# Dense matrix products as eight 64x32 tiles in an attention-and-feed-forward kernel on one Trainium2 core

## The chip, the core and the metric

The kernel runs on one core of a Trainium2 chip. The metric is the device time of one execution in microseconds, as the median of several runs. A profile is one further execution, taken apart by the hardware profiler; it has its own time, and its span runs from its first to its last instruction.

The engines are named as in the profile: PE is TensorE, and PEld its weight loads; DVE is VectorE, ACT ScalarE, POOL GpSimd, and SP is SyncE, which here issues most DMAs. A matrix product takes a stationary operand (the weights, loaded by a weight load) and a moving operand that is streamed past it. Its sums go to one of eight PSUM banks. The array of 128x128 cells can be used as smaller tiles that work beside each other: 64x128 means two tiles of 64 rows, 64x32 means eight tiles, 32x64 eight of another shape.

## The reference

The input x has 2048 rows of 448. It is normalized by row, and a sliding attention and a feed-forward network both read the normalized rows. Their product is added to x.

```python
def _A_ref(x, wqkv, wo):                 # H = 16 heads of 28
    W, dil = 8, 2
    qkv = (x @ wqkv)...                   # 448 -> 3*448
    idx = pos[:, None] - (jnp.arange(W) * dil)[None, :]
    logits = einsum("bhsd,bhswd->bhsw", q, k[idx]) * Dh ** -0.5   # masked where idx < 0
    o = einsum("bhsw,bhswd->bhsd", softmax(logits), v[idx])
    return o.reshape(B, S, D) @ wo
def _B_ref(x, w1, b1, w2, b2):            # 448 -> 1792 -> 448
    return gelu(x @ w1 + b1) @ w2 + b2
xn = _layernorm(x)
return x + _A_ref(xn, ...) * silu(_B_ref(xn, ...))
```

All data is bfloat16. Since the attention looks back in steps of two, even and odd rows never meet; the kernel keeps all even rows first and all odd rows after them.

## The kernel before

The 2048 rows are 16 tiles of 128 (index t) in four chunks of 512 (index c). Attention works in nine blocks (VIS) of four windows of 57 queries (56 in the middle block), each window with 64 keys.

The kernel doesn't write its order down by hand. Every step is a task with an engine, a cost, its dependencies, the buffers that it takes and gives back, and a priority. `_Plan.run` simulates the engines with these costs and picks, among the tasks that can start nearly first, the one with the highest priority; the tasks are then emitted in the order found. HOP (0.10 us) is the planner's time from one engine to another, and SWITCH (0.095 us) what it charges when PE goes to another tile shape (`mode`). The priorities are tables of numbers (PRIO, LATER). PE, like every engine, works through its tasks in the emitted order.

The steps on PE are these. `project` makes q, k and v: `qk_rows` (L532) and `vproj` (L556). `ff1` (L591) makes the first layer, 128 hidden units for 512 rows at a time, and ACT applies gelu (L595). Both have a contraction of 448 = 3.5 x 128. They run in `pair`, as row halves: two products share the array, one on rows 0 to 63 into one bank and the other on rows 64 to 127 into another bank; then the halves are swapped, and each product is finished in the same bank by the other half of the rows. Between the two phases a `nop` on POOL or SP waits for the last products of the first phase, and the second phase waits for the `nop`, since two row halves must not write one bank at the same time. `ff2_part` (L627) makes the second layer for one row tile with 14 products of 128x128, and `final_part` (L796) the output projection with four of them. The last row tile is worked in two halves of 224 columns.

Scores (L677) are 64 small products of 57 columns in tiles of 32x64, into four banks. P V (L709) is 64 products of 57 columns in tiles of 64x32, into two banks. `VISITS` joins them: a visit is P V of one block and, right behind it, the scores of the block two further on. Between scores and P V lie the exponential on ACT (L687) and the mask (L693), which the planner gives to DVE or POOL. After P V, DVE turns the sums (L719), inverts the row sums (L723), turns them back (L728) and multiplies (L733).

After the second layer come the bias (L649, DVE), tanh (L655, ACT) and the gate (L659, DVE); after the projection the product with the gate (L801, DVE), the sum with x (L807, DVE or POOL for the first eight row tiles, DVE for the others) and the output's DMA on SP (L811). POOL issues the DMAs that gather v for the blocks (L354), and SP the transposing loads of the normalized rows and of q and k (L360).

Of the kernel before, what the change touches and what calls it, by code (L numbers as in the profile page):

```python
# [16 lines left out]
SWITCH = 0.095  # L17
TILED = 30
SAME = 20
HOPS = ("POOL", ("SP", "POOL"))  # L20
MASK_ON = (("DVE", "POOL"), (0.4, 1.2))


def VISITS(bs):
    out = [[("S", b)] for b in bs[:2]]
    for i, b in enumerate(bs):
        out.append([("P", b)] + [("S", c) for c in bs[i + 2:i + 3]])
    return out
# [11 lines left out]
class _Task:  # L40
    __slots__ = ("eng", "cost", "deps", "fn", "prio", "take", "give", "slots",
                 "start", "end", "on", "ndep", "users", "tail", "seq", "table", "limit", "mode", "out")


class _Plan:
# [7 lines left out]
    def add(self, eng, cost, fn, deps=(), prio=0, take=(), give=(), tail=0.0, table=(), limit=None,  # L53
            mode=128):
# [5 lines left out]
        t.mode, t.out = mode, None  # L60
# [14 lines left out]
    def _at(self, t, e, free):  # L75
        at = free.get(e, 0.0)
        for p, n in t.take.items():
            if len(p.free) < n or p.fifo and p.fifo[0] is not t:
                return None
            at = max(at, sorted(p.free)[n - 1][0] + HOP)  # L80
        if t.table and self.table not in t.table:
            at += TABLE
        for d in t.deps:
            at = max(at, d.end - d.tail if d.on == e else d.end + HOP)
        if e == "PE" and t.mode != self.mode:
            at = max(at, free.get(e, 0.0) + SWITCH)
        return at

    def run(self):
# [6 lines left out]
        self.mode = 128  # L96
        ready = [t for t in self.tasks if not t.ndep]
        order = []
        while ready:
# [14 lines left out]
            tiled = first[2] == "PE" and self.mode < 64  # L114
            at, t, e, c = min(near, key=lambda k: (-k[1].prio - (TILED if tiled and k[1].mode < 64 else SAME if k[2] == "PE" and k[1].mode == self.mode else 0),
# [4 lines left out]
            if e == "PE" and t.fn is not None:  # L120
                self.mode = t.out or t.mode
# [43 lines left out]
def kernel(  # L165
# [80 lines left out]
    def ring(name, n, shape, dt=BF16, fifo=False):  # L246
# [24 lines left out]
        "project": (49.5, 205, 104, 52.5,),  # L271
        "project2": (147, 150, 101, 61,),
        "values": (89.5, 62.5, 21, 58,),
        "attn": (185, 179.5, 78, 174.5, 106.5, 106, 138.5, 136.5, 32.5,),
        "ff1": (185, 180, 84.5, 176.5, 66.5, 64.5, 156.5, 189.5, 203, 146, 76, 114.5, 77.5, 179.5,
            75.5, 118.5, 180.5, 14.5, 163, 68, 151, 115.5, 194.5, 167.5, 180, 188.5, 86, 93,),
        "gelu": (62.5, 22.5, 95, 92.5,),
        "ff2": (144, 162.5, 103.5, 142.5, 44.5, 112.5, 67, 5, 89, 106.5, 101.5, 75, 74, 55, 11.5,
            6.5,),
        "final": (140, 19.5, 70.5, 47, 112, 34.5, 23.5, 142.5, 73, 53, 198.5, 188.5, 81.5, 126.5,  # L280
            180, 71,),
        "norm": (37.5, 132, 179.5, 129.5, 74.5, 99, 161, 69, 63, 62, 43.5, 73, -5.5, 90, 133.5,
            150,),
        "loads": (166.5, 166, 188, 139.5, 54.5,),
        "stats": (47.5, -60, 180.5, 23, 127, 56, 188.5, 77, 197.5, -13.5, 185, 205.5, 138, 14, 52.5,
            138.5,),
        "turn_x": (108.5, -1, 28, 116, 210, 116.5, 131.5, 160, 41.5, 79.5, 70, 119, -4.5, 74.5,
            132.5, 111,),
        "turn_qk": (68.5, 112, 174.5, 90, 80, 6, 149.5, 60.5, 4, 140.5, 199.5, 96.5, 103, 166.5,
            140, 156,),  # L290
        "move_v": (81.5, 95, 23, 95, 18.5, 26.5, 8, 128, 29.5,),
        "copies": (50, 119.5, 58.5, 76, 32.5, 135.5, 43, 1, 87, 79.5, 129, 77, 32, 41.5, 135,),
    }
    LATER = {"swap": 135, "qk": 165, "v": 29.5, "gelu": 30.5, "exp": 55.5, "mask": -60, "pv": 45, "recip": -16.5, "os": 54.5, "y": 153.5, "tanh": 182.5, "g": 58, "sg": 183, "o": 120.5}
# [50 lines left out]
    def dma(eng, dst, src, kb, prio, deps=(), issue=0.5, rate=350.0):  # L345
# [3 lines left out]
        return plan.add("DMA", kb / rate, lambda _: None, [a], prio, tail=1.7)  # L349
# [16 lines left out]
    def load_x(t0, n, prio, eng="SP", deps=()):  # L366
        d = dma(eng, x_sb[:, t0:t0 + n, :],
                rows(x_half, t0 * P, n * P).rearrange("(t p) d -> p t d", p=P), 112 * n, prio, deps,
                rate=270.0 if t0 < TPC else 350.0)
# [11 lines left out]
    def load_w(kt, prio):  # L381
        t_w.append([dma("SP", w_in[:, kt, :], A_wqkv[kt * P:(kt + 1) * P, :], 336, prio, rate=270.0)])
# [6 lines left out]
    t_w.append([dma("SP", w_in3[:64], tails[:, 0:3:2, :], 112, PRIO["loads"][3], rate=270.0),  # L389
                dma("SP", w_in3[64:], tails[:, 1:3, :], 112, PRIO["loads"][3], rate=270.0)])  # L390

    t_b1z = plan.add("POOL", 0.1, memset("gpsimd", b1r[:], 0.0), [t_on], prio=99)
    t_b1r = dma("POOL", b1r[:NMT], B_b1.rearrange("(m f) -> m f", f=P), 4, 94.5, [t_b1z])
    t_b1r.tail = 5.0
# [74 lines left out]

    def together(top, bottom):  # L470
        return [(f(), g()) for f, g in zip(top, bottom, strict=True)]
# [5 lines left out]
    def pair(a, b, prio, early=False):  # L477
# [11 lines left out]
        def f2(k):  # L489
            held["told"] = (nc.gpsimd if k.on == "POOL" else nc.sync).nop()  # L490
            for i in held["last"]:
                behind(held["told"], i)
        told = plan.add(HOPS[0] if early else HOPS[1], 0.06, f2, [t], 300)

        def f3(k):
            p, q = buf(p_b, t, 0), buf(p_b, t, 1)
            for i in together([part(b, q, kt, 0, kt + 4) for kt in range(3)], [part(a, p, kt, 1, kt + 4) for kt in range(3)])[0]:
                behind(i, held["told"])
# [5 lines left out]
    def first_batch(tiles, prio, tiles0=0):  # L504

        f = []
        for kt in range(3):
            for i, js in enumerate(tiles):
                def f1(k, kt=kt, i=i, js=js):
                    for q, j in enumerate(js):  # L510
                        j.part(buf(p_b, f[i] if kt else k, q), kt, 2, kt == 0, False)
# [14 lines left out]
    def qk_rows(t, which, prio):  # L526
        cs = slice(t * P, (t + 1) * P)

        def part(ps, kt, half, start, stop):
            r = half_rows(half)  # L530
            w = w_in[r, kt, which * D:(which + 1) * D] if kt < 3 else w_in3[r, 0, :]
            return nc.tensor.matmul(ps[:, :D], xnT[r, kt, cs], w, start=start, stop=stop)  # L532

        def evac(a, own, i):
# [6 lines left out]
            if len(t_row[t]) == 2:  # L541
                t_qk[t] = dma_T(qkT[:, :, :, cs].rearrange("p w g c -> p (w g) c"), lambda: b[:].rearrange("p w h c -> p (w h c)"),
                                t_row[t], PRIO["turn_qk"][t], None, 2, 1.9 if t < 3 else 3.8 if t == TPC else 2.0 if t == TPC + 1 else 1.27)
# [6 lines left out]
    def vproj(t, prio):  # L550
        k0 = t * P

        def part(ps, kt, half, start, stop):
            r = half_rows(half)
            w = w_in[r, kt, 2 * D:] if kt < 3 else w_in3[r, 1, :]
            return nc.tensor.matmul(ps[:, :D], xnT[r, kt, k0:k0 + P], w, start=start, stop=stop)  # L556
# [7 lines left out]
    def values(b):  # L564

        t_v[b], v_at[b] = [], []
        for i in range(2):
            first = None
            for w in range(2):
                k0 = VIS[b][2][w][i][1]  # L570
                for lo in sorted({k0, max(k0, (k0 + NK - 1) // P * P)}):
# [6 lines left out]
                    t_v[b].append(d)  # L578
# [6 lines left out]
    def ff1(c, mt, prio, gate):  # L585
# [3 lines left out]
        def part(ps, kt, half, start, stop):  # L589
            r = half_rows(half)  # L590
            return nc.tensor.matmul(ps[:], w1[r, kt, ms], xnT[r, kt, cs], start=start, stop=stop)  # L591
# [18 lines left out]

    def ff2(t, prio):
        t_g[t] = []
        for cs, n, end in parts(t):
            ff2_part(t, cs, n, end, prio - 0.1 * end)

    def ff2_part(t, cs, n, end, prio):
# [23 lines left out]
        a = halves[1]  # L640
        t_f2[t] = a

        if t == NT - 1:
            prio += 9
        if biased:
            y, pool, held = halves[0], p_b, ((p_b, halves[0], 0),)
        else:
            def f2(k):
                nc.vector.tensor_tensor(out=buf(p_y, k)[:, :n], in0=buf(p_b, halves[0])[:, :n], in1=b2[:, cs], op=ALU.add)  # L649
            y, pool = plan.add("DVE", dve(n), f2, [a, t_b2], prio + LATER["y"], take=(p_y,), give=((p_b, halves[0], 0),)), p_y  # L650
# [15 lines left out]
    def scores_of(b):  # L666
        q, nq, wins = VIS[b]

        def fn(banks):
            for i in range(2):  # L670
                for g in range(G):
                    for hl in range(4):
                        for w in range(2):
                            r = slice(32 * hl, 32 * hl + 32)
                            q0, k0 = wins[w][i]
                            c0 = (G * i + g) * nq
                            nc.tensor.matmul(banks[hl][NK * w:NK * w + NK, c0:c0 + nq], qkT[r, 1, g, k0:k0 + NK],  # L677
                                             qkT[r, 0, g, q0:q0 + nq], start=True, stop=True)
# [288 lines left out]
```

## Time and profile before

| | |
|---|---|
| median of three runs | 157.52 us (157.37 to 158.0) |
| the profiled execution | 157.98 us |
| its span | 156.2 us |
| TensorE clock granted | 1.00 throughout |
| PE busy | 150.1 us, 2204 products |
| DVE, ACT, POOL busy | 113.2, 83.3, 74.7 us |

The lines of the profile give the source line, the engine, the operation, the tiles written and read, the shape and the count. For products, "64*128 64x512" is the tile shape and the moving operand. In a timeline, a line begins with the start and the length in us of a merged stretch. Products overlap, and their ends are modelled, so the step from one to the next is read from the starts. In a line of the windows view the columns are the stretch, its length and each engine's busy time with its number of instructions.

### The profile page before, as it was taken

How to read it: one execution, taken by the hardware profiler on the slowest of the kernel's cores; microseconds unless marked ns; L12 is line 12 of the kernel's file. 1: busy time of each engine (PE TensorE's matmuls, PEld its weight loads, DVE VectorE, ACT ScalarE, POOL GpSimd, SP SyncE). 2: the span in 40 equal slices, each digit the busy share in tenths (PEclk: the TensorE clock that was granted, in tenths of full speed). 3: DMA queues.
4: the chain of work that ended last, by engine and by line, in shares of the span. 5: the costliest groups of instructions: out<-in, count | busy, mean ns of one | idle time of the engine just before them, and what ended most of it. 6: DMA issues, size and time to landing. Idle time of an engine off the chain costs nothing.

```text
span 156.2 us, 5305 instructions
## 1 busy us (share of the span) xinstructions
PE 150.1 (96%) x2204; PEld 77.8 (50%) x2204; DVE 113.2 (72%) x259; ACT 83.3 (53%) x149; POOL 74.7 (48%) x123
## 2 busy tenths in 40 slices
PE   6999999999999999999999999999999999999980
PEld 2544454444455555455554644455556444545570
DVE  4789551486266758997799895109899996998992
ACT  3245867378889416444634149782496587051220
POOL 7854856000459408839261098389599780000000
PEclk9999999999999999999999999999999999999999
DMA  4999969999749443099039822123300100200211
GB/s 156 329 317 315 167 124 187 237 269 307 141 95 166 64 82 90 10 192 138 4 83 85 131 70 73 38 76 83 105 0 4 34 31 29 63 4 0 68 36 43
DMA packets 33575, 17.36 MB, mean 111 GB/s; under 512 B 25331, under 2 KB 32387, under 8 KB 33552
## 3 DMA queue, kind: packets, MB, share of 16 engines
q1 hardware_dynamic: 31472, 14.03, 41.3%
q0 software_dynamic: 1936, 2.88, 8.5%
q8 instruction: 17, 0.28, 0.8%
q10 hardware_dynamic: 144, 0.11, 0.2%
q14 instruction: 6, 0.05, 0.1%
HBM read 7.06 MB, written 1.84 MB: 57 GB/s over the span
## 4 chain that ended last, share of the span: by engine, by line
PE 80%; DVE 8%; DMA 3%; POOL 2%; issue 2%; ACT 1%; SPq 1%; DVEq 0%; ACTq 0%; POOLq 0%
PE bank L627 23%; PE bank L591 22%; PE bank L532 11%; PE bank L796 7%; PE bank L556 6%; PE bank L677 4%; PE bank L709 4%; PE bank L327 3%; DMA xnT<-xn 3%; POOL v L354 2%; DVE sg L801 2%; DVE o L807 1%; DVE w_in L659 1%; ACT E L687 1%; DVE xn L438 1%
## 5 line engine op out<-in xcount | busy, mean ns | idle before, releaser
L627 PE MATMUL bank<-w,h 128*128 128x448 bf16 (+1 forms) x238 | 45.2, 342 | 0.0
L591 PE MATMUL bank<-xnT,w 64*128 64x512 bf16 x392 | 44.7, 376 | 0.0
L595 ACT ACTIVATE h<-bank,b 128x512 bf16<-128x512 f32 x56 | 34.0, 689 | 12.9 <-PE bank L591 12.8
L354 POOL DMA_DIRECT2D v<-v_tok x52 | 27.6, 538 | 19.8 <-PE bank L709 9.0
L693 POOL TENSOR_TENSOR E<-E,m_gen 128x456 bf16<-128x456 bf16 x24 | 26.7, 1139 | 11.7 <-ACT E L687 9.5
L627 PEld LDWEIGHTS <-h 128*128 128x128 bf16 x238 | 22.3, 98 | 18.1 <-issue 0.4
L591 PEld LDWEIGHTS <-w 64*128 64x128 bf16 x392 | 19.1, 94 | 22.7 <-issue 1.1
L532 PE MATMUL bank<-w_in,xnT 64*128 64x448 bf16 (+1 forms) x212 | 24.3, 350 | 0.1
L687 ACT ACTIVATE E<-bank 128x456 bf16<-128x456 f32 (+1 forms) x36 | 17.0, 555 | 9.1 <-PE bank L677 9.1
L655 ACT ACTIVATE t<-y 128x448 f32<-128x448 f32 x15 | 8.7, 578 | 17.4 <-DVE y L649 17.4
L719 DVE STREAM_TRANSPOSE dt<-bank 128x480 f32<-128x480 f32 (+1 forms) x18 | 12.1, 671 | 5.6 <-PE bank L709 5.6
L532 PEld LDWEIGHTS <-xnT 64*128 64x128 bf16 (+1 forms) x212 | 10.6, 94 | 10.9 <-issue 1.1
L314 DVE CAST qk_tok<-bank 128x448 bf16<-128x448 f32 x16 | 9.4, 613 | 6.8 <-PE bank L532 6.8
L796 PE MATMUL bank<-wo,oT 128*128 128x448 bf16 (+1 forms) x68 | 14.1, 342 | 0.0
L312 ACT CAST qk_tok<-bank 128x448 bf16<-128x448 f32 x16 | 8.3, 533 | 10.6 <-PE bank L532 10.0
L556 PE MATMUL bank<-w_in,xnT 64*128 64x448 bf16 (+1 forms) x106 | 13.4, 349 | 0.0
L649 DVE TENSOR_TENSOR y<-bank,b 128x448 f32<-128x448 f32 x15 | 9.3, 620 | 4.9 <-PE bank L627 4.9
L728 DVE STREAM_TRANSPOSE dt<-rd 128x480 f32<-128x480 f32 (+1 forms) x18 | 12.1, 673 | 0.5
L733 DVE TENSOR_TENSOR oT<-bank,dt 128x456 bf16<-128x456 f32 (+1 forms) x18 | 11.3, 630 | 0.5
L404 DVE BATCH_NORM_STATS2 st<-x_sb 128x6 f32<-128x448 bf16 x16 | 9.6, 603 | 2.4 <-DMA x_sb<-in_A_x_dram 2.4
L438 DVE TENSOR_SCALAR xn<-x_sb,mv,rstd 128x448 bf16<-128x448 bf16 x16 | 6.3, 394 | 6.0 <-POOL rstd L426 5.8
L796 PEld LDWEIGHTS <-oT 128*128 128x128 bf16 x68 | 6.3, 98 | 6.3 <-issue 0.8
(62 smaller groups left out, 128.9 us busy)
## 6 DMA issues: line engine op xcount, KB each, us to landing
out_dram<-o SPq DMA_DIRECT2D x15, 112.0 KB, 1.7
w<-in_B_w_dram SPq DMA_DIRECT2D x2, 784.0 KB, 7.2
w<-in_B_w_dram SPq DMA_DIRECT2D x2, 672.0 KB, 7.0
x_sb<-in_A_x_dram SPq DMA_DIRECT2D x3, 448.0 KB, 6.3
v<-v_tok POOLq DMA_DIRECT2D x20, 64.0 KB, 2.5
w_in<-in_A_wqkv_dram SPq DMA_DIRECT2D x3, 336.0 KB, 4.3
w<-in_B_w_dram SPq DMA_DIRECT2D x4, 112.0 KB, 6.5
wo<-in_A_wo_dram POOLq DMA_DIRECT2D x4, 98.0 KB, 4.2
```

Source lines behind the costliest of these rows:

```text
L354: nc.gpsimd.dma_start(dst(k), src())
L532: return nc.tensor.matmul(ps[:, :D], xnT[r, kt, cs], w, start=start, stop=stop)
L556: return nc.tensor.matmul(ps[:, :D], xnT[r, kt, k0:k0 + P], w, start=start, stop=stop)
L591: return nc.tensor.matmul(ps[:], w1[r, kt, ms], xnT[r, kt, cs], start=start, stop=stop)
L595: nc.scalar.activation(buf(p_h, own, i)[:], buf(p_b, own, i)[:], ACT.Gelu_apprx_tanh, bias=b1[:, mt:mt + 1])
L627: nc.tensor.matmul(ps[:, :n], buf(*h_at[(c, mt)])[:, j * P:(j + 1) * P], w2[:, mt, cs], start=(mt == 0 and not biased), stop=(mt == NMT - 1))
L687: nc.scalar.activation(buf(p_E, k)[:, :n], buf(p_b, a, at + hl)[:, :n], ACT.Exp, scale=SCALE)
L693: (nc.gpsimd if k.on == "POOL" else nc.vector).tensor_tensor(out=E[:, :n], in0=E[:, :n], in1=m[:, :n], op=ALU.mult)
L719: nc.vector.transpose(buf(p_dt, k)[:, :32 * m], buf(p_b, po, i)[:, :32 * m])
L728: nc.vector.transpose(buf(p_dt, d)[:, :32 * m].rearrange("p (b c) -> p b c", c=32), buf(p_rd, r)[:, :m].unsqueeze(2).to_broadcast((P, m, 32)))
L733: nc.vector.tensor_tensor(out=oT[:, :, q0:q0 + 2 * nq], in0=buf(p_b, po, i)[:, :n].rearrange("p (l q) -> p l q", l=4), in1=buf(p_dt, d)[:, ...
L796: nc.tensor.matmul(ps[:, :n], oT[:, kt, t * P:(t + 1) * P], wo[:, kt, cs], start=(kt == 0), stop=(kt == KT - 1))
```

## The change

Nearly all products with a contraction of 64 rows or more now run in the tile shape of P V. `strips` cuts the 128 output columns of a product into four products of 32, and `together` issues those of the two row halves in turn, so that one round is eight products in eight tiles. The second layer and the output projection, which used the whole array, are worked for two row tiles at a time in two phases with the swap and the `nop` of `pair` (`rows_in_pairs`, `ff2_pair`, `final_pair`). The last two row tiles keep the 128x128 form, and so does the first batch of projections except for its last step. The `nop` waits for the last product alone, and only the first product of the second phase waits for the `nop`.

Scores and P V are tasks of their own (`scores`, `attend`), with no fixed order between them but the data; the planner adds APART (0.25 us) when one comes right behind the other, and prefers tasks of the shape that PE has. All masks go to DVE. The sum with x of row tile 14 and of the first half of 15 goes to POOL. The bias of the first layer is loaded earlier, the planner's rates for the first loads are a little higher, and all priorities are new.

```diff
@@ -15,17 +15,11 @@
 SLACK = 0.12
 TABLE = 1.28
 SWITCH = 0.095
-TILED = 30
+APART = 0.25
+OTHER = 0
 SAME = 20
 HOPS = ("POOL", ("SP", "POOL"))
-MASK_ON = (("DVE", "POOL"), (0.4, 1.2))
-
-
-def VISITS(bs):
-    out = [[("S", b)] for b in bs[:2]]
-    for i, b in enumerate(bs):
-        out.append([("P", b)] + [("S", c) for c in bs[i + 2:i + 3]])
-    return out
+MASK_ON = ("DVE", 0.4)
 
 
 class _Pool:
...
@@ -84,7 +78,16 @@
             at = max(at, d.end - d.tail if d.on == e else d.end + HOP)
         if e == "PE" and t.mode != self.mode:
             at = max(at, free.get(e, 0.0) + SWITCH)
+        if e == "PE" and t.thin and self.thin:
+            at = max(at, free.get(e, 0.0) + APART)
         return at
+
+    def same(self, e, t):
+        if e != "PE":
+            return 0
+        if t.mode == self.mode:
+            return SAME
+        return OTHER if self.mode == 32 and t.mode != self.dense else 0
 
     def run(self):
         for t in self.tasks:
...
-            tiled = first[2] == "PE" and self.mode < 64
-            at, t, e, c = min(near, key=lambda k: (-k[1].prio - (TILED if tiled and k[1].mode < 64 else SAME if k[2] == "PE" and k[1].mode == self.mode else 0),
+            at, t, e, c = min(near, key=lambda k: (-k[1].prio - self.same(k[2], k[1]),
                                                    k[0], k[1].seq))
             if t.limit is not None and at > t.limit:
                 t.fn, c = None, 0.0
             t.on, t.start = e, at
             if e == "PE" and t.fn is not None:
-                self.mode = t.out or t.mode
+                self.mode, self.thin = t.mode, t.thin
+                self.dense = t.mode if t.mode != 32 else self.dense
             if t.table and self.table not in t.table:
                 self.table = t.table[0]
             free[e] = at + c
...
     t_b1z = plan.add("POOL", 0.1, memset("gpsimd", b1r[:], 0.0), [t_on], prio=99)
-    t_b1r = dma("POOL", b1r[:NMT], B_b1.rearrange("(m f) -> m f", f=P), 4, 94.5, [t_b1z])
-    t_b1r.tail = 5.0
+    t_b1r = dma("POOL", b1r[:NMT], B_b1.rearrange("(m f) -> m f", f=P), 4, 400, [t_b1z], tail=4.3)
...
@@ -467,8 +469,15 @@
     def half_rows(half):
         return slice(64 * half, 64 * half + 64) if half < 2 else slice(0, P)
 
+    def strips(out, lhsT, rhs, half, start, stop):
+        n = P if half > 1 else 32
+        return [lambda c=c: nc.tensor.matmul(out[c:c + n], lhsT[:, c:c + n], rhs, start=start, stop=stop) for c in range(0, P, n)]
+
     def together(top, bottom):
-        return [(f(), g()) for f, g in zip(top, bottom, strict=True)]
+        done = []
+        for f, g in zip(top, bottom, strict=True):
+            done.append([q() for pair in zip(f(), g(), strict=True) for q in pair])
+        return done
 
     def behind(later, earlier):
         tc.add_manual_dep(later.ins, earlier.ins.name,
@@ -488,14 +497,12 @@
 
         def f2(k):
             held["told"] = (nc.gpsimd if k.on == "POOL" else nc.sync).nop()
-            for i in held["last"]:
-                behind(held["told"], i)
+            behind(held["told"], held["last"][-1])
         told = plan.add(HOPS[0] if early else HOPS[1], 0.06, f2, [t], 300)
 
         def f3(k):
             p, q = buf(p_b, t, 0), buf(p_b, t, 1)
-            for i in together([part(b, q, kt, 0, kt + 4) for kt in range(3)], [part(a, p, kt, 1, kt + 4) for kt in range(3)])[0]:
-                behind(i, held["told"])
+            behind(together([part(b, q, kt, 0, kt + 4) for kt in range(3)], [part(a, p, kt, 1, kt + 4) for kt in range(3)])[0][0], held["told"])
...
-            return nc.tensor.matmul(ps[:], w1[r, kt, ms], xnT[r, kt, cs], start=start, stop=stop)
+            return strips(ps[:], w1[r, kt, ms], xnT[r, kt, cs], half, start, stop)
...
+    def rows_in_pairs(A, B, steps, deps, prio, n, take, give, dep2=()):
+
+        def part(f, half, i):
+            return lambda: f(half, i)
+        ph1, ph2, held = [], [], {}
+        for i, own in enumerate(steps):
+            def f1(k, i=i, own=own):
+                p, q = buf(p_b, (ph1 or [k])[0], 0), buf(p_b, (ph1 or [k])[0], 1)
+                held["last"] = together([part(A(p), 0, m) for m in own], [part(B(q), 1, m) for m in own])[-1]
+            ph1.append(plan.add("PE", pe(n, len(own)), f1, deps[i] + ph1[-1:], prio + 0.5 * i, take=() if i else (p_b, p_b), tail=0.15, mode=64))
+
+        def f2(k):
+            held["told"] = (nc.gpsimd if k.on == "POOL" else nc.sync).nop()
+            behind(held["told"], held["last"][-1])
+        told = plan.add(HOPS[1], 0.06, f2, ph1[-1:], 300)
+        for i, own in enumerate(steps):
+            def f3(k, i=i, own=own):
+                p, q = buf(p_b, ph1[0], 0), buf(p_b, ph1[0], 1)
+                first = together([part(B(q), 0, m) for m in own], [part(A(p), 1, m) for m in own])[0]
+                if not i:
+                    behind(first[0], held["told"])
+            end = i + 1 == len(steps)
+            ph2.append(plan.add("PE", pe(n, len(own)), f3, [told] + ph2[-1:] + list(dep2) * end, prio + LATER["swap"] + 0.5 * i,
+                                give=give if end else (), tail=0.15, mode=64))
+        return ph1[0], ph2[-1]
+
     def ff2(t, prio):
-        t_g[t] = []
-        for cs, n, end in parts(t):
-            ff2_part(t, cs, n, end, prio - 0.1 * end)
+        t_g.setdefault(t, [])
+        if t >= NT - 2:
+            for cs, n, end in parts(t):
+                ff2_part(t, cs, n, end, prio - 0.1 * end)
+        elif t % 2 == 0:
+            ff2_pair(t, prio)
+
+    def ff2_pair(t, prio):
+        c, j = divmod(t, TPC)
+
+        def product(u):
+            def at(ps):
+                def f(half, mt):
+                    r = half_rows(half)
+                    first = (half == u % 2) and mt == 0
+                    last = (half != u % 2) and mt == NMT - 1
+                    return strips(ps[:, :D], buf(*h_at[(c, mt)])[r, (u % TPC) * P:(u % TPC) * P + P], w2[r, mt, :], half, first, last)
+                return f
+            return at
+        last = j == TPC - 2
+        own, a = rows_in_pairs(product(t), product(t + 1), (range(7), range(7, NMT)),
+                               ([t_h[(c, mt)] for mt in range(7)] + t_w2[0] + [ff1_last[c]], [t_h[(c, mt)] for mt in range(7, NMT)] + t_w2[1]),
+                               prio, D, 2, tuple(h_at[(c, mt)] for mt in range(NMT)) if last else (), [t_f2[q] for q in range(c * TPC, t)] if last else ())
+        t_f2[t] = t_f2[t + 1] = a
+        t_g[t + 1] = []
+        for i in range(2):
+            gate(t + i, slice(0, D), D, own, i, a, prio, False)
...
+    last_visit = {"S": None, "P": None}
+
+    def visit(what, fn, deps, prio, n, give):
         def f1(k):
-            for fn in fns:
-                fn(k)
+            for i in range(2):
+                fn([buf(p_b, k, j) for j in range(n)], i)
+        a = plan.add("PE", 0.5, f1, deps[0] + deps[1] + [last_visit[what]], prio, take=(p_b,) * n, give=give[0] + give[1], tail=0.15,
+                     mode=32 if what == "S" else 64, thin=True)
+        last_visit[what] = a
+        return a, a
+
+    def scores(b, early, gate):
+        fn, deps = scores_of(b)
         prio = PRIO["attn"][b]
-        a = plan.add("PE", cost, f1, deps, prio + (LATER["pv"] if what[0][0] == "P" else 0), take=take, give=give, tail=0.15,
-                     mode=32 if what[0][0] == "S" else 33)
-        a.out = 32 if what[-1][0] == "S" else 33
-        at, exps = 0, []
-        for w, blk in what:
-            last_visit[w].append(a)
-            if w == "S":
-                state[blk] = weights_of(blk, a, at, PRIO["attn"][blk], state["gate"])
-                exps += state[blk][0]
-                at += 4
-            else:
-                for w in range(2):
-                    output_of(blk, a, at + w, w, PRIO["attn"][blk])
-                at += 2
-        return exps
-
+        a, z = visit("S", fn, [d + early for d in deps], prio, 4, ((), ()))
+        return weights_of(b, a, z, prio, gate)
+
+    def attend(b, exps, masked):
+        fn, give = values_of(b, exps)
+        prio = PRIO["attn"][b]
+        a, z = visit("P", fn, [masked + t_v[b][0], t_v[b][1]], prio + LATER["pv"], 2, (tuple(v_at[b][:1]), give + tuple(v_at[b][1:])))
+        for w in range(2):
+            output_of(b, a, z, w, prio)
...
     def final(t, prio):
+        if t < NT - 2:
+            if t % 2 == 0:
+                final_pair(t, prio)
+            return
         for i, (cs, n, end) in enumerate(parts(t)):
             final_part(t, cs, n, t_g[t][i], prio - 0.1 * i)
+
+    def final_pair(t, prio):
+        def product(u):
+            def at(ps):
+                def f(half, kt):
+                    r = half_rows(half)
+                    return strips(ps[:, :D], oT[r, kt, u * P:(u + 1) * P], wo[r, kt, :], half, half == u % 2 and kt == 0, half != u % 2 and kt == KT - 1)
+                return f
+            return at
+        own, a = rows_in_pairs(product(t), product(t + 1), (range(KT),), (t_oT[t] + t_oT[t + 1] + t_wo + [t_f2[t]],), prio, D, 2, ())
+        for i in range(2):
+            close(t + i, slice(0, D), D, t_g[t + i][0], own, i, a, prio)
...
-        o = plan.add(("DVE", "POOL") if t < 2 * TPC else "DVE", (dve(n, 2), 1.15) if t < 2 * TPC else dve(n, 2), f3, [s], prio + LATER["o"], take=(p_o,), give=((p_sg, s, 0),))
+        o = plan.add("POOL" if t == NT - 2 or t == NT - 1 and not cs.start else ("DVE", "POOL") if t < 2 * TPC else "DVE",
+                     0.1 + n / 420 if t == NT - 2 or t == NT - 1 and not cs.start else (dve(n, 2), 1.15) if t < 2 * TPC else dve(n, 2), f3, [s], prio + LATER["o"], take=(p_o,), give=((p_sg, s, 0),))
...
-                state["gate"], state["early"] = gels, gels[:-1]
-                for what in visits(run):
-                    exps += attn(what[0][1], what)
+                done = [(b, *scores(b, gels[:-1], gels)) for b in run]
+                for b, e, m in done:
+                    attend(b, e, m)
+                    exps += e
```

The calls of `qk_rows` and `vproj` are changed as that of `ff1` (its two lines with `ps[:]` above). The tables PRIO and LATER have new numbers throughout, which are left out here.

## The prediction

> **What bounds the kernel now.** I read the page first.
>
> ```profile
> PE 150.1 (96%) x2204; PEld 77.8 (50%) x2204; DVE 113.2 (72%) x259; ACT 83.3 (53%) x149; POOL 74.7 (48%) x123
> ...
> q8 instruction: 17, 0.28, 0.8%
> ...
> PE 80%; DVE 8%; DMA 3%; POOL 2%; issue 2%; ACT 1%; SPq 1%; DVEq 0%; ACTq 0%; POOLq 0%
> ```
>
> TensorE is busy for 96% of the span and carries 80% of the chain that ended last. The waits of PE add to 0.2 us after its start. So a gain must come out of PE's own order and modes, and a loss must make PE slower or make it wait. The timeline of PE shows what its time is made of:
>
> ```profile
> 84.85 1.69 PE L796 MATMUL bank<-wo,oT 128*128 128x448 bf16 x8
> 86.38 1.49 PE L627 MATMUL bank<-w,h 128*128 128x448 bf16 x7
> 87.79 0.68 PE L709 MATMUL bank<-E,v 64*32 64x57 bf16 x64
> 88.40 0.78 PE L677 MATMUL bank<-qkT 32*64 32x57 bf16 x64
> 89.11 1.50 PE L627 MATMUL bank<-w,h 128*128 128x448 bf16 x7
> 90.45 0.92 PE L796 MATMUL bank<-wo,oT 128*128 128x448 bf16 x4
> 91.30 0.93 PE L556 MATMUL bank<-w_in,xnT 64*128 64x448 bf16 x8
> ```
>
> Read the starts. Eight products of 128x128 take 86.38 - 84.85 = 1.53 us, 0.19 each (448 columns). The seven after them take 1.41, where 7 x 0.19 = 1.33: the step into the 64x32 shape costs some 0.09. The four L796 at 90.45 take 0.85 instead of 0.76 before the shape 64x128: again 0.09. I use 0.095 for a change of tile shape. P V costs 0.61 and the scores behind it 0.71, the step out included. A scores visit that stands alone is cheaper:
>
> ```profile
> 48.94 0.70 PE L677 MATMUL bank<-qkT 32*64 32x57 bf16 x64
> 49.57 8.12 PE L627 MATMUL bank<-w,h 128*128 128x448 bf16 x42
> ```
>
> That is 0.63 from start to start. How fast the array takes 64x32 tiles is seen at the head of a P V visit, in a narrow window of the timeline (73.36 to 73.491):
>
> ```profile
> 73.37 0.30 PE L709 MATMUL bank<-E,v 64*32 64x57 bf16 x32
> ```
>
> 32 products, four rounds of eight tiles, each tile with its own weights, began in 0.12 us: 30 ns a round. 57 columns stream in 57/448 x 189 = 24 ns, so weight loads and issue together cost at most 6 ns a round beyond the stream. A whole visit has 64 in 0.61 us, at worst 9.5 ns each, 76 ns for eight.
>
> Then the windows by stage, for the engine that may come next:
>
> ```profile
> core 0: us, PE busy (x) PEld busy (x) DVE busy (x) ACT busy (x) POOL busy (x), PEclk, DMA share, GB/s
> ...
> 62.00:92.00 30.00, 30.00 (x594) 16.00 (x590) 27.03 (x51) 12.94 (x26) 14.90 (x16) 1.00 0.59 94
> ...
> 104.00:153.40 49.40, 47.47 (x794) 26.12 (x788) 43.45 (x80) 23.57 (x41) 20.80 (x26) 1.00 0.14 41
> ```
>
> DVE is at 90% from 62 to 92 and at 88% from 104 to its last instruction; from 144.68 on the chain of waits runs through it. It has little room.
>
> **Part 1, mode changes.** Following the tile shapes down the PE timeline from 45 us to the end I count 37 changes. After: only scores leave the 64x32 shape (nine visits, two steps each, 18), and the last two row tiles' second layer and output projection keep 128x128 (one step in, one reserve): 20. 17 x 0.095 = -1.6 us. If the planner mixes the last two tiles with other work, some steps come back; if two scores visits touch, two go. The start, until 13 us, keeps its five.
>
> **Part 2, scores and P V apart.** P V had a step in and was followed by scores. Scores behind P V took 0.69, 0.75, 0.63, 0.71 and 0.63 against 0.63 alone: 0.25 us in all. The second of two P V visits in a row, at 104.63 and 132.52, took 0.15 more each than 0.61 less its step. Apart, both go: -0.55 us.
>
> **Part 3, the dense work as eight tiles.** 392 and 300 row-tiled products (196 and 150 rounds), 196 of the second layer's (14 of 16 tiles) and 56 of the output projection become 598 rounds of eight, some 6,040 products in all instead of 2,204. A round streams the same columns as the step it replaces: 189 ns, or 216 for 512 columns. The trace has no such tile with a long stream. From below I know no reason why a round should be faster than its stream: 0. From above: 6 ns a round, as P V shows at most, is 3.6 us. I take 0, since the 6 ns were seen where a load must fit into 24 ns, and here it has 187. Issue needs 76 ns a round and is hidden by the stream of 187. Instructions: 0.28 MB in 17 blocks is 16 KB, 256 instructions; 0.8% of 16 engines' span is 1.2 us a block. After, a block lasts 16 rounds, 3.0 us, so fetching has 2.5-fold room; scores alone already eat half a block in 0.63 us with no wait. Nothing. But a visit leaves the queue empty, and the next dense round then starts its eighth tile 60 ns late (76 less what two tiles need), which is paid when the shape is next drained: nine scores visits, +0.5 us.
>
> One rule speaks against this part. By the Trainium skill (TensorE: Matmul & The Clock Gate, Back-to-back and "Wait — 56ns"), matmul starts never come closer than about 25 ns; eight would need 200 ns, 11 more than a 448-column step, and over 402 such rounds the sum would be 4.4 us worse. The row above, 32 starts in 0.12 us, does not agree, and the measurement decides. The same skill (TensorEngine Tiling, Restrictions) says that column tiling switches off the fast weight load, and the page named before it (LDWEIGHTS) gives columns/1.2 ns for one load, 27 ns for 32 columns: eight strictly in turn would be an estimated 213 ns, 24 more, 9.6 us in the 402 rounds. Again the window, with 32 loads and products in 0.12 us, says otherwise.
>
> **Part 4, the swap of row halves.** Second layer and projection now run in two phases, with a hop over SP or POOL between (14 new ones). The first layer and the projections have such hops, and PE shows no wait at any, since other work is put between; the cover is other PE work of the same shape. Uncovered, a hop is two semaphore steps at the planner's 0.1 (HOP) and its nop's 0.06, 0.26; 14 of them are 3.6 us. If SP is in a transposing load's issue (1.21 us in the chain) or POOL in an issue of v (0.54), everything queued on PE behind the swap waits as long, and so would the evacuations on DVE and ACT. I take 0, because the plan has 2.6 us phases to interleave, and keep 0 to 3.6. A pair now holds two banks for 5.3 us where one was held for 2.65, of eight, and scores need four at once; I put this with the slow cases.
>
> **Part 5, the masks go to DVE.** L693 ran 28 times on POOL (1.05 us median) and 8 times on DVE (0.39). 28 x 0.39 = +10.9 us of DVE. Against it, DVE's own two-input steps were stretched while POOL masked:
>
> ```profile
> 113.86 1.11 DVE L659 SCALAR_TENSOR_TENSOR w_in<-t,y 128x448 bf16<-128x448 f32 x1 [0.31 <-ACT t L655]
> ...
> 116.14 1.23 DVE L659 SCALAR_TENSOR_TENSOR w_in<-t,y 128x448 bf16<-128x448 f32 x1
> ```
>
> Undisturbed it takes 0.62. Five such steps after 113 us and one at 63 give back 3.5 us. Two last adds (L807, 0.39 and 0.28) move to POOL, -0.67. Net +6.8: from 45 us to the end DVE would hold 93.8 of some 106.5 us, 88% instead of 80%. In 62 to 92, 14 masks put 27.0 to 32.5 in 30, but ten casts there (5.8 us) may run on ACT, which is busy 12.9, and adds of the early tiles may go to POOL. I cost it at nothing on the path, with PE as cover; the bound without cover is the second rival. Loads, priorities and the earlier bias load only change the planner's order; the first 13 us I leave as they are.
>
> **The sum.** -1.6 - 0.55 + 0.5 = -1.65. DVE's end of the chain loses some 0.1 to 0.6 by the two adds; I take 0.1. The profiled execution had 157.98 (span 156.2), so 156.2; the median of the runs lies 0.46 lower: 155.8.
>
> **Rivals.** (a) The gain is eaten: a third of the hops uncovered (1.3 us), or one ns a round (0.6) and half the returned steps (0.8). Then about 157.2. For it: PE has few idle engines to lean on and the order is wholly new. Against: nothing waited so far. (b) DVE becomes the bound, slower than before. Place: from 104 us to the end. There 13 of the masks add 5.1, contention gives back 2.95 (113.86, 116.14, 118.69, 123.83, 124.72), the adds 0.67: +1.5 on a DVE with 5.9 us idle. It decides if those idle times are waits for P V and gates that cannot be filled, so that DVE's work ends 1.5 later: 159.0; with bank waits of the same kind up to 160.5. Against: no casts are left late, but the idle is four times the addition. (c) The array does not stream long columns in eight tiles at full rate, since four column tiles read the same operand four times. If the rate is only what 57 columns in 30 ns show, a round takes 1.25 times as long, 47 ns on 189, 54 on 216: 402 x 47 + 196 x 54 = 29.5 us, 185; at a quarter of that, 163. It decides when a round takes over 192 ns, where the 17 steps are used up. Against: 30 ns may be issue alone, as the next 32 products are slower still. (d) The change does not do as it says if the planner still alternates shapes; it then lies in (a).
>
> **Chances.** What a measurement of this kernel can tell from no change is about 0.5%, 0.8 us: under 156.7 is faster, over 158.3 slower. The forecast 0.56 (own range 154.2 to 156.7, the lower end if DVE's end shifts by all of 0.6 and the new order also saves the 0.56 us hole at 114 us), (a) 0.16, (b) 0.17, (c) 0.11. Faster 0.56, same 0.16, slower 0.28. The range from 154.2 to 160.5 holds all but (c) and a few hundredths on either side.
>
> **What would show it.** Right: some 20 shape changes after 45 us; dense rounds of eight at 189 and 216 ns; P V at about 0.5 us without a step; L693 all on DVE, L659 at 0.62 throughout; PE idle no more than now. Wrong: rounds over 192 ns; PE waits on DVE for banks or on a nop at the swaps; DVE over 95% from 104 us on with PE done early.

## The result, and the profile after

The changed kernel takes 211.9 us at the median of four runs (209.67 to 216.15), against 157.62 for the kernel before: a ratio of 1.333, 95% interval 1.326 to 1.340. The ratios in this document leave out executions over 1.5% above the fastest of the same kernel (here 213.13 and 216.15), so they can lie below those of the medians. The forecast was 155.8, its range ended at 160.5, and even the rival of slow streams at full size (185 us) lies far below. The profiled execution took 210.67 us.

These lines of its page answer to those shown of before: the span, the engines, the fetches of instructions, the engines' shares of the chain that ended last, and two of the costliest groups. L474 is the product in `strips`, L734 that of the scores and L765 that of P V.

```profile
span 208.9 us, 12993 instructions
...
PE 160.0 (77%) x6042; PEld 94.4 (45%) x6042; DVE 115.1 (55%) x272; ACT 86.4 (41%) x157; POOL 50.1 (24%) x102
...
q8 instruction: 47, 0.77, 1.6%
...
PE 73%; issue 20%; DMA 3%; SPq 1%; DVE 1%; DVEq 0%
...
L474 PE MATMUL bank<-w,h 64*32 64x448 bf16 x1568 | 46.5, 350 | 14.2 <-issue 14.2
L474 PE MATMUL bank<-xnT,w 64*32 64x512 bf16 x1568 | 49.9, 382 | 6.7 <-issue 6.5
```

PE went from 96% busy to 77%, and no engine took its place: DVE stands at 55%. 20% of the chain is "issue", time in which PE waited for nothing that the profile shows. The products number 6,042, where 6,040 were forecast, and the fetched instruction blocks 47, where the kernel before fetched 17. The timeline of PE shows where the idle time sits; the bracket at a line's end is the idle time before it.

```profile
104.52 0.71 PE L765 MATMUL bank<-E,v 64*32 64x57 bf16 x41
106.51 0.28 PE L765 MATMUL bank<-E,v 64*32 64x57 bf16 x23 [1.28 <-issue]
106.60 2.81 PE L474 MATMUL bank<-w,h 64*32 64x448 bf16 x105
110.23 0.38 PE L474 MATMUL bank<-w,h 64*32 64x448 bf16 x7 [0.82 <-issue]
110.55 0.70 PE L734 MATMUL bank<-qkT 32*64 32x57 bf16 x64
111.18 1.68 PE L474 MATMUL bank<-w,h 64*32 64x448 bf16 x57
113.96 1.51 PE L474 MATMUL bank<-w,h 64*32 64x448 bf16 x55 [1.10 <-issue]
```

Count products from hole to hole. From 106.51 to 110.23 there are 23 + 105 = 128; from 110.23 to 113.96, 7 + 64 + 57 = 128. Each product has a weight load, so a hole comes every 256 instructions, whatever the shape: it splits a P V visit as it splits the second layer. 0.77 MB in 47 fetches is 16 KB each, and 12,084 products and loads in 47 fetches are 257 each, so one fetch brings one such block. Between the holes the dense rounds keep 189 and 216 ns from start to start of every eighth product, the full stream rate. The exception is twelve rounds behind the longest hole, from 39.17 us on: at half the granted clock they take 373 and 426 ns, some 2 us more in all. Over the whole trace 43 of 47 block ends come late, by 51.5 us in all beyond the normal spacing to the start eight products before. The span grew by 52.7; that the two numbers nearly agree is partly chance, since the half clock comes on top and the rest of the order changed as well.

The fetches tell when: the hole that ends at 113.96 had its block's fetch begin at 111.37 and end at 112.53; the next fetch began at 115.00, ended at 115.87, and PE went on at 117.42. So the turn of a block is here 1.0 to 1.1 us from PE's going on to the next fetch, 0.9 to 1.2 us of transfer, and 1.4 to 1.5 until PE goes on.

### The profile page after: what moved, and what is told of

The parts are those of the page before. It is cut to its first block, busy times and chain, and to the rows that moved or that the text cites. A ratio compares the mean times of both kernels' runs of the same rounds, so it can differ in the third digit from the quotient of the medians.

```text
span 208.9 us, 12993 instructions
## 1 busy us (share of the span) xinstructions
PE 160.0 (77%) x6042; PEld 94.4 (45%) x6042; DVE 115.1 (55%) x272; ACT 86.4 (41%) x157; POOL 50.1 (24%) x102
## 4 chain that ended last, share of the span: by engine, by line
PE 73%; issue 20%; DMA 3%; SPq 1%; DVE 1%; DVEq 0%
PE bank L474 64%; PE bank L765 3%; PE bank L734 3%; DMA w_in<-in_A_wqkv_dram 3%; PE bank L684 3%; SPq L350 1%; PE bank L844 1%; DVE sg L851 0%; PE bank L455 0%; DVE w_in L717 0%; DVE o L857 0%; PE bank L682 0%; DVEq L851 0%
## 5 line engine op out<-in xcount | busy, mean ns | idle before, releaser
L474 PE MATMUL bank<-w,h 64*32 64x448 bf16 x1568 | 46.5, 350 | 14.2 <-issue 14.2
L474 PE MATMUL bank<-xnT,w 64*32 64x512 bf16 x1568 | 49.9, 382 | 6.7 <-issue 6.5
L474 PE MATMUL bank<-w_in,xnT 64*32 64x448 bf16 (+1 forms) x1218 | 40.9, 360 | 12.9 <-issue 12.6
L474 PEld LDWEIGHTS <-h 64*32 64x32 bf16 x1568 | 23.2, 92 | 31.0 <-issue 20.3
L474 PEld LDWEIGHTS <-w 64*32 64x32 bf16 x1568 | 25.3, 93 | 25.6 <-issue 11.6
L474 PEld LDWEIGHTS <-xnT 64*32 64x32 bf16 (+1 forms) x1218 | 21.5, 94 | 27.5 <-issue 18.7
L775 DVE STREAM_TRANSPOSE dt<-bank 128x480 f32<-128x480 f32 (+1 forms) x18 | 12.1, 674 | 16.8 <-PE bank L765 13.5
L857 POOL TENSOR_TENSOR o<-x_sb,sg 128x448 bf16<-128x448 bf16 (+1 forms) x7 | 7.0, 1014 | 54.3 <-DVE sg L851 30.4
L474 PE MATMUL bank<-wo,oT 64*32 64x448 bf16 x448 | 14.2, 350 | 2.2 <-issue 2.2
L750 DVE TENSOR_TENSOR E<-E,m_gen 128x456 bf16<-128x456 bf16 x28 | 11.1, 412 | 2.5 <-ACT E L744 1.9
L474 PEld LDWEIGHTS <-oT 64*32 64x32 bf16 x448 | 7.7, 93 | 6.9 <-issue 3.6
```

The costliest lines, as they stand in the source:

```text
L474: return [lambda c=c: nc.tensor.matmul(out[c:c + n], lhsT[:, c:c + n], rhs, start=start, stop=stop) for c in range(0, P, n)]
L750: (nc.gpsimd if k.on == "POOL" else nc.vector).tensor_tensor(out=E[:, :n], in0=E[:, :n], in1=m[:, :n], op=ALU.mult)
L775: nc.vector.transpose(buf(p_dt, k)[:, :32 * m], buf(p_b, po, w)[:, :32 * m])
```

## The experiments

Theory A: a block of 256 PE instructions can't be had faster than one turn of its fetch. Theory B: eight narrow tiles stream or load more slowly (my rival (c)). Theory C: the order, the hops or the masks.

**The rate by itself.** Five stretches of one shape each:

```python
def rounds(n, cols, count=160):
    for _ in range(count):
        for c in range(0, P, n):
            for h in range(2):
                r = slice(64 * h, 64 * h + 64)
                nc.tensor.matmul(banks[h][c:c + n, :cols], a[r, c:c + n], b[r, :cols], start=True, stop=True)
```

> A kernel of PE work alone: five stretches of 160 rounds (eight tiles of 64x32, four of 64x64 or two of 64x128, 448 columns; then 64x32 with 512 and with 57 columns), parted by full-array products; it computes nothing of the reference. Theory A (instruction supply: a block of 256 PE instructions cannot be had in less than about 3.4 to 3.8 us, since the fetch of the next one starts only when its predecessor is begun): 64x128 and 64x64 at 189 ns a round, 30 us; 64x32 holds 10 blocks, so about 36 us with 448 columns, 36 with 512, and also some 35 with 57 columns, with holes 256 instructions apart. Theory B (the array streams long columns slower in eight tiles): 64x32 evenly slower, over 200 ns a round without holes, and 57 columns at 66 to 76 ns a round, 11 to 12 us.

From first start to the next stretch's, 160 rounds took 30.4 us in 64x128, 30.4 in 64x64, 34.5 in 64x32 with 448 columns, 35.3 with 512 and 33.3 with 57; the last three are 0.7 to 1.7 us below what A gave. Columns hardly matter in 64x32: an eighth of the work takes nearly the same time. The beginning of the last stretch, a piece of the third, and all of the second:

```profile
180.62 1.94 PE L62 MATMUL bank<-b,a 64*32 64x57 bf16 x215
184.94 1.21 PE L62 MATMUL bank<-b,a 64*32 64x57 bf16 x128 [2.39 <-issue]
188.39 1.27 PE L62 MATMUL bank<-b,a 64*32 64x57 bf16 x128 [2.24 <-issue]
191.85 1.27 PE L62 MATMUL bank<-b,a 64*32 64x57 bf16 x128 [2.19 <-issue]
```

```profile
100.70 3.22 PE L62 MATMUL bank<-b,a 64*32 64x448 bf16 x128 [0.21 <-issue]
104.15 3.22 PE L62 MATMUL bank<-b,a 64*32 64x448 bf16 x128 [0.23 <-issue]
```

```profile
54.17 30.46 PE L62 MATMUL bank<-b,a 64*64 64x448 bf16 x640
```

In both 64x32 stretches, 128 products begin every 3.45 us, now and then every 3.73 or 4.00. Theory A's turn is thus 3.45 us at the least with quiet queues, 13.5 ns an instruction. It was the same at both granted clocks, 1.00 in the 448-column stretch and 0.50 in the other from 186.5 us on. A block of 448-column rounds wants 3.02 and waits; one of 512 columns wants 3.45 and nearly fits (160 rounds of 216 ns would be 34.6 us). Theory B falls: the narrow tiles are not slow, and 64x64, with 8 instructions a round, has no hole at all.

**The same instructions without narrow tiles.** The kernel before, with the first layer alone cut into strips of 32 output columns, and then with the first layer in its old 64x128 tiles, but each product cut into four of 128 moving columns. Both have 16 instructions a round.

```diff
-            return nc.tensor.matmul(ps[:], w1[r, kt, ms], xnT[r, kt, cs], start=start, stop=stop)
+            return strips(ps[:], w1[r, kt, ms], xnT[r, kt, cs], half, start, stop, 32)      # ff1_only
+            return [lambda n=n: nc.tensor.matmul(ps[:, n:n + P], w1[r, kt, ms],             # ff1_cols
+                    xnT[r, kt, c * CH + n:c * CH + n + P], start=start and not n, stop=stop and n == CH - P)
+                    for n in range(0, CH, P)]
```

> The kernel before with only the first layer cut into strips of 32 columns. 196 rounds of 512 columns hold 3136 instructions, 12 blocks more or less. A block lasts 16 x 216 = 3.45 us there. Theory A: if a block takes 3.6 us, +0.15 each, and up to 0.4 where the fetch is slow or other work of PE eats a block faster: 2 to 8 us slower, with holes at block ends in the first layer alone. Theory B: 216 ns become 216 x 1.25 or more, over 10 us slower, evenly. Theory C: no change.

> The kernel before with the first layer's products in their old tiles of 64x128, but each cut into four of 128 moving columns: 16 instructions a round, as many as in ff1_only, and no narrow tile. Streams alone would be 4 x 55.8 = 223 ns a round instead of 216, +1.5 us over 196 rounds. Theory A (instruction supply, 3.45 us for a block of 256): holes at block ends as in ff1_only, 6 to 12 us slower. Theory B (narrow tiles stream or load slowly): +1 to 3 us and no holes.

Measured: 1.0599 times before (1.0508 to 1.0689) and 1.0612 (1.0568 to 1.0656), both nearly 10 us slower. In the second kernel the late starts at block ends hold some 6.4 us, and its rounds, which stream 4 x 128 columns, take 223 ns instead of 216, 1.4 us in all. The same number of instructions costs nearly the same without one narrow tile, and with holes, which settles it against B; and this kernel has the old order, which settles it against C. The first layer of the second kernel:

```profile
31.41 4.96 PE L598 MATMUL bank<-xnT,w 64*128 64x128 bf16 x171
37.61 3.75 PE L598 MATMUL bank<-xnT,w 64*128 64x128 bf16 x128 [1.24 <-issue]
42.71 5.41 PE L598 MATMUL bank<-xnT,w 64*128 64x128 bf16 x181 [1.35 <-issue]
```

For ff1_only I had expected 2 to 8 us, and that was a miss on the low side. I had spread a mean turn over the extra blocks. Its late starts at block ends hold some 7 us: scores, P V and the first layer meet in one block, and early fetches come late (the one before 37.89 began some 3.5 us after PE had gone on). And one hole of 2.0 us idle was followed by TensorE at half clock:

```profile
34.00:38.00 4.00, 1.99 (x74) 0.89 (x66) 3.83 (x11) 2.02 (x4) 0.00 (x0) 1.00 1.25 212
39.20:42.50 3.30, 3.30 (x72) 1.76 (x64) 0.00 (x0) 2.22 (x4) 0.00 (x0) 0.50 1.23 197
```

These are stretches of ff1_only in the windows view; the column after the five engines is the granted clock, 1.00 and then 0.50. Eight rounds took 426 ns instead of 216 there, 1.7 us in all. The same is seen behind the longest hole of the changed kernel:

```profile
39.17 2.42 PE L474 MATMUL bank<-w_in,xnT 64*32 64x448 bf16 x43 [4.89 <-issue]
```

```profile
39.20:43.50 4.30, 4.30 (x96) 2.09 (x104) 1.78 (x5) 0.53 (x1) 1.07 (x2) 0.50 0.45 77
```

Not every long idle time has this effect: in strips64, the first kernel of the next experiment, PE waits 3.78 us for a load, and the granted clock stays at 1.00.

**Fewer instructions in the new order.** The changed kernel, its emitted order untouched, with strips of 64 and of 128:

```diff
-        n = P if half > 1 else 32
+        n = P if half > 1 else 64     # strips64
+        n = P                         # strips128
```

> The changed kernel, its order unchanged, with dense strips of 64 output columns, four tiles a round: half the dense instructions, 8 a round. Theory A: a block lasts 6.0 us in dense work, longer than its fetch, so the holes go and the time is 156 to 161 us, with P V's step into its own shape (18 steps, 1.7 us) now paid. Theory B: two column tiles instead of four, perhaps half of the loss: 180 to 190. Theory C (the new order, the swap hops or the masks on DVE cost the time): still over 200.

> The changed kernel, its order unchanged, with dense strips of all 128 columns, two tiles a round as before in the row-half products. It tells what the new order is worth without the narrow tiles. Theory A and B: 156 to 160 us, with 18 steps into and out of P V's shape that the planner did not count. Theory C: still over 200.

Measured: strips64 1.0491 (1.0381 to 1.0601), 167.75 us at the median; strips128 1.0141 (1.0059 to 1.0223), 161.27. Before was 158.24 in the same comparison. So of the 54 us all but three go when the instructions go. C had over 200 and falls as the cause of the loss. Both are above what A gave them. On strips128, whose span is 3.2 us longer than before, two waits account for 2.3:

```profile
28.25 2.25 PE L474 MATMUL bank<-w_in,xnT 64*128 64x448 bf16 x22 [0.84 <-DMA xnT<-xn]
...
46.01 0.81 PE L474 MATMUL bank<-xnT,w 64*128 64x512 bf16 x6
48.25 0.93 PE L474 MATMUL bank<-w_in,xnT 64*128 64x448 bf16 x8 [1.42 <-DMA xnT<-xn]
```

In both PE waited for transposing loads of the normalized rows. The new order asks for them at a time when the queues are fuller: the DMA share was 1.20 from 44.3 to 48.3 us, against 0.52 before in 44 to 48. On strips64 the second wait was 3.78 us, and two block ends cost 1.4 more. Why that load lands later there was not settled, and the rest of both differences was not traced; some 18 steps into and out of P V's shape, 1.7 us at 0.095 each, may be part of it.

**Fetches beside loads.** 57-column and 448-column stretches in quiet, then both again while 16 MB are loaded:

```diff
+    def load():
+        for k in range(12):
+            nc.sync.dma_start(big[:, k % 2, 0:3, :], B_w1[0:384, :].rearrange("(k p) c -> p k c", p=P))
```

> A kernel of PE work alone, nothing of the reference: 160 rounds of eight 64x32 tiles with 57 columns, then with 448, both in quiet; then both again while 16 MB of weights are loaded on the other queues. Theory A, with fetches that share the DMA engines: 33 and 34.5 us in quiet, and 4 to 5 us a block, 40 to 50 us, under the load, which would explain the 3.8 us a block of the changed kernel. If the fetch has a path of its own: no difference.

The 57-column stretch took 35.1 us in quiet, its blocks 3.45 to 4.0 us each, and 49.0 with the load. While the load lasted, a block took 5.6 to 7.0 us, more than the 4 to 5 that I had expected; then 3.45 again:

```profile
127.86 1.27 PE L62 MATMUL bank<-b,a 64*32 64x57 bf16 x128 [4.38 <-issue]
133.78 1.27 PE L62 MATMUL bank<-b,a 64*32 64x57 bf16 x128 [4.65 <-issue]
140.79 1.27 PE L62 MATMUL bank<-b,a 64*32 64x57 bf16 x128 [5.75 <-issue]
144.25 1.27 PE L62 MATMUL bank<-b,a 64*32 64x57 bf16 x128 [2.19 <-issue]
```

The second 448-column stretch fell behind the load's end, 36.4 against 36.0, and says nothing. The packets of the fetches tell where the time went: under the load each still took 0.93 to 0.96 us, but began 3.3 to 4.6 us after PE had gone on, against 1.0 to 1.6 in quiet. So a fetch waits while the queues are full, as it would if it shared the DMA engines with the load. That fits the changed kernel: from its third to its last fetch, 172 us, it used 44 blocks, 3.9 us each (over the whole trace the ten turns up to 60.8 us, in the time of the loads, take 4.9 on average, the others 3.7). The fetch before its longest hole (4.89 us idle, before 39.17) began 5.7 us after PE had gone on, while the DMAs moved up to 388 GB/s, and took 0.92 us.

**A try for a better version.** With the planner given measured costs for the visits, its span for the kernel before comes to 156.1 us, where the profile had 156.2. With these costs I searched priorities anew, for the wide row pairs with separate visits and, as a control, for the kernel before.

```diff
+        n = P                                                          # wide_retuned, in strips
+                     mode=32 if what == "S" else 33, thin=True)       # P V has its own shape
+        a = plan.add("PE", 0.52, f1, ...)                              # and APART = 0.12
+            cost += 0.57 if n else 0.525                               # before_retuned, in attn
```

> The changed kernel with dense strips of all 128 columns (as strips128), and its planner told so: P V has a shape of its own, scores and P V visits cost 0.52 us and 0.12 more behind each other, transposing loads land 0.3 us later; priorities searched anew for the planner's span. Planner's span 153.5 us, against 156.1 for the kernel before when its visits are given their measured cost. Theory A (the narrow tiles' instructions were the whole loss; the row pairs, the separate scores and P V and the masks on DVE are harmless): 153.5 to 157 us. If the new order has a cost of its own, as on strips128: 159 to 162.

> The kernel before, unchanged in its work, with measured costs for scores and P V visits, transposing loads 0.3 us later and priorities searched in the same way: the control that tells the row pairs' part from the search's. Planner's span 154.1 us. Theory A with a gain from the search alone: 154 to 157.5. If planning has no room left: 157 to 159.

Measured: 1.0193 (1.0159 to 1.0227) and 1.0029 (1.0003 to 1.0055). Both miss the planner's spans, with 159.5 and 157.0 us in the profiles. For the wide version this is the second case of what was expected, a cost of the new order's own. It again loses in the first 62 us: PE has waits of 1.1 us for a hop on SP, 0.8 for a load of weights and 0.4 for a transposing load. In the control PE waits 1.4 us for DVE at 118.8. So no version here beats the kernel before, and whether the row pairs are worth anything once the early loads are in time stays open.

## Why the prediction was wrong

The step that failed is the term "Instructions" in Part 3. I saw that a block of 256 would be used up in 3.0 us and set against it 1.2 us, the time that a block's packet is on the wire. What had to be set against it is the whole turn from one block to the next: 3.45 us at the least in quiet, about 6 beside loads. The term "Issue" beside it fails with it: instructions came at 13.5 ns each at best, which is 216 ns for the 16 of a round and not 76, and a stream of 189 doesn't hide that. "Nothing" measured 51.5 us. That is the size of the miss; its direction did not hang on this term alone, since strips128, with no such hole to speak of but some 18 more shape steps (1.7 us), was 1.4% slower than before and not faster.

The evidence that I took for it did not bear on it. "Scores alone already eat half a block in 0.63 us with no wait": half a block at a time is the point, since the kernel before then returns to wide products, 2 instructions for 189 ns, and the turn of the next block passes unseen. What PE has ready probably covers it: the first 32 products of a P V visit, with their loads, start within 0.12 us and the others 8.3 ns apart, from which I estimate that some 64 instructions lie ahead. In wide products these are 6 us of work, more than a turn; in eight tiles they are four rounds, 0.76 us. No run tests this explanation by itself. The kernel before fetched 17 blocks in 156 us, one in 9, and nobody waited for them. I never compared the demand, 256 instructions in 3.0 us over many blocks on end, with any stretch that had been sustained.

The Trainium skill (Runtime: NRT & Kernel Launch, Instruction fetch mechanics) has the block of 16 KiB, and the runs agree: 0.77 MB in 47. It calls the cost of crossing a block "mostly hidden", since instructions are handed out more slowly than blocks arrive. The runs say the opposite for PE: 8.3 ns for a product with its load, from start to start in a P V visit, against 27 ns that the turn allows.

Point by point. Part 1 cannot be seen in the time, but the steps are gone: the tile shape changes 19 times after 45 us, where 20 were forecast. P V at 155.84 took 0.52 us, as forecast; four other visits that no block end splits took 0.60 to 0.74, so the gain there was not had throughout. Part 2 holds as far as separate scores cost 0.63.

In Part 3 the stream was right: 189 and 216 ns a round between holes at the full clock, so that both rules of the Trainium skill that Part 3 weighs (a floor of 25 ns between products, no fast weight load) have no effect here, and rival (c) with its rate of 57 columns in 30 ns was wrong as well; it had the sign by a mechanism that these rounds do not show. The late eighth tile did not show after the nine scores visits, where it started 23 ns after the first; after some P V visits it came 58 to 146 ns late, and the rounds kept their rate.

Part 4: no swap shows a wait of its own in the changed kernel, though with PE idle for a fifth of the time that is a weak test; on strips128, with its busy PE, there is none either, and the one of 1.1 us in wide_retuned is the only one seen; there SP was in a transposing load's issue (1.26 us in the chain), the case that Part 4 names.

Part 5: on strips128 the late gates take 0.62 us at the median where they took 1.07 (one still 1.46), the masks 0.39, and DVE is busy for 114.6 us, 1.4 more than before and not 6.8, since the planner gave casts to ACT and adds to POOL. It did not become the bound there, PE has no wait for it after its start, and rival (b) did not come. "Loads, priorities and the earlier bias load only change the planner's order" was an error of its own: the new order waits 2.3 us for transposing loads on strips128, more than the 1.65 that I had it gain.

## What to carry to other kernels

Count instructions per microsecond on the engine that bounds, not only its busy time. In these runs PE could use 256 instructions (128 products with their loads) every 3.45 us at best, and every 6 or so beside heavy loads; the stretches below that rate had no holes, and in those above it nearly every block left one. So a finer tiling that keeps the stream time and multiplies the instructions by four is free only in short visits between wide products. When a profile offers a packet's duration as the cost of a fetch, don't take it for the whole: it was near 1 us in quiet and under load alike. Look for the distance between two fetches in a stretch that does nothing else, or measure it.

## What the runs showed of the hardware

The holes come at exact multiples of 256 instructions, at products and weight loads alike, and PE goes on 1.2 to 1.7 us after the packet's end. Four 64x64 tiles stay under the limit with 8 instructions a round: 160 rounds took 30.4 us, as in 64x128. And a long hole can cost twice: after 2.0 us of idle in ff1_only, and after 4.89 us in the changed kernel, the granted clock was 0.50 for 3.4 and 4.3 us of work, though not after 3.78 us in strips64.
